# A decode block on one core: the last chunk of the down projection split into three blocks instead of two, with two of the sums made on VectorE

## The chip, the cores and the metric

The kernel runs on one core of a Trainium2 chip. The metric is the time of one execution on the device in microseconds (us); three executions of the kernel before gave 265.24 (the median), 265.24 and 265.53 us.

## What is computed

One decode step of a transformer block for a batch of 8 tokens, all in float32: layernorm, attention over the last 1024 positions of a cached sequence (32 query heads, 4 key/value heads), the output projection, a residual, a second layernorm, a gated GELU layer and a second residual.

```python
B, Sq, D = 8, 1, 1024;  Hq, Hkv, Sk, Dh = 32, 4, 4096, 128;  Df = 3584
W = min(4096, max(256, Sk // 4))                      # 1024
q = (layernorm(x) @ wq) split into 32 heads
p = softmax(q @ k_cache[:, :, Sk - W:].T * Dh ** -0.5);  o = p @ v_cache[:, :, Sk - W:]
h = x + o @ wo
n = layernorm(h)
out = h + (gelu(n @ w_gate) * (n @ w_up)) @ w_down    # w_down: 3584 x 1024
```

## The kernel before

All weights and the cache are read once, in the order of use: query weights, keys, values, output weights, gate and up weights, down weights. Each piece is one DMA on SyncE's queue into a ring in SBUF, and TensorE works on a piece when its semaphore says that it has landed. The order of instructions on each engine is the order in which the program writes them: `run` appends a computation to an engine with the waits that it needs, `move` appends a DMA to a queue (SyncE's unless another is named).

The batch has only 8 rows, so a matmul uses 32 columns of the array. The kernel always keeps four *groups* at work: group r writes PSUM partitions 32r to 32r+31, and matmuls of different groups run side by side.

The down projection (from L410 on) multiplies the activations `at` (28 chunks of 128 of the 3584 inner columns) by the 28 row chunks of `w_down`, each 128 x 1024. The chunks come in loads of 8, 8, 4, 4, 2 and 1 (`PARTS`, `wd0` to `wd5`, L424 to L443); the eight small `w_side` loads carry a part of chunk 19. The last chunk, number 27, comes in blocks of its own (`ENDS`, `we0` and `we1`, L446 to L449). The program writes the loads of the end in the order `wd4`, `wd5`, `we0`, `we1`.

Chunks are taken in pairs at L462: two chunks times two halves of 512 columns give four matmuls of 512 columns, one for each group, all into the bank `ya`. `first = DF // P - TAIL` is 26: pairs go up to chunks 24 and 25. Then VectorE copies `ya` to SBUF (`d1`, L476). What is left is summed in another layout, in which group j holds the output columns 256j to 256j+255. `add` (L481) issues it for two halves of 128 of these columns, the first in bank `acc`, the second in bank `tb`; so it issues eight matmuls of 128 columns. It is called for chunk 26 and then for `d1` with the constant `add2`, which folds the four groups of `ya` into the new layout. Chunk 27 follows at L497, four matmuls for each block. ScalarE copies each half to `o_fin` (L500), and two DMAs store it, `out0` on SyncE's queue (after one more wait for a VectorE memset, L503) and `out1` on ScalarE's.

After that SyncE waits until ScalarE has issued its store, clears the semaphores (L514) and waits for both stores to land (L516).

```python
for q in range(first, last):
    add(lambda j: at[:, q, :], lambda j: rows_of(q)[:, j * QW:(j + 1) * QW], arrived[q], at_ok[1],
        start=(q == first))
add(lambda j: add2[:, j // 2, :], lambda j: d1[:, (j % 2) * QW:(j % 2) * QW + QW], d1_ok)
```

Of the kernel before, what the change touches and what calls it, by code (L numbers as in the profile page):

```python
# [37 lines left out]
class Flow:  # L38
# [42 lines left out]
    def run(self, engine, make, *waits, mark=True):  # L81
        ins = self.start(engine, make, waits)
        if not mark:
            return None
        self.done[engine] += 1
        ins.then_inc(self.own[engine], 1)
        return self.own[engine], self.done[engine]

    def move(self, name, out, src, *waits, engine="sync"):
        s = self.sem(name)  # L90
        self.start(engine, lambda e: e.dma_start(out, src), waits).then_inc(s, 16)  # L91
        return s, 16


def decode_block(nc, x, wq, kt, v, wo, gu, dn, side, ends, outs):
# [9 lines left out]
    run, move = fl.run, fl.move  # L105
# [4 lines left out]
    def sb(name, *shape):  # L110
        return nc.alloc_sbuf_tensor(name, list(shape), F32).ap()
# [15 lines left out]
    def load(src, name, letters, **sizes):  # L127
# [9 lines left out]
    ta, tb, ya = bank("ta", N), bank("tb", N), bank("ya", N)  # L137
    acc = bank("acc", N)
# [12 lines left out]
        out=ident, in_=ident, compare_op=ALU.not_equal, fill=1.0, base=0,  # L151
# [76 lines left out]
    for hf in range(2):  # L228
        w, w_in, wb = wq_t[hf]
        q_ps = (acc, tb)[hf]  # L230
        for c in range(NC):
            for j in range(NQ):
                tok = run("tensor", lambda e, c=c, j=j: e.matmul(  # L233
                    q_ps[32 * j:32 * j + 32, :], xt[c], w[:, c, j * N:(j + 1) * N],
                    start=(c == 0), stop=(c == NC - 1)),
                    w_in, x_ok, mark=(c == NC - 1 and j == NQ - 1))
        free[wb] = tok
        q_sb = sb(f"q{hf}", P, N)
        tok = run("vector", lambda e: e.tensor_scalar(q_sb, q_ps, scale, None, op0=ALU.mult), tok)
        acc_free = tok  # L240
        qt, tok = transposes(ta, q_sb, N // P, tok, ta_free)
# [10 lines left out]
    for hf in range(2):  # L252
        s_ps = big[hf]
        k_t, k_in, wb = load(kt[hf], f"kt{hf}", "s b k", s=2, b=B)
        for b in range(HB):
            for k0 in range(0, W, N):
                for r in range(NQ):
                    s, half = divmod(r, 2)
                    c0 = 32 * b + 160 * half
                    end = b == HB - 1 and k0 + N == W and r == NQ - 1  # L260
                    tok = run("tensor", lambda e: e.matmul(  # L261
                        s_ps[32 * r:32 * r + 32, k0:k0 + N], qz[hf][:, s, c0:c0 + 32],
                        k_t[:, s, half * HB + b, k0:k0 + N],
                        start=(b == 0), stop=(b == HB - 1)), k_in, q_ok[hf], mark=end)
# [31 lines left out]
    for hf in range(2):  # L296
        p_sb, p_ok, share, sh_ok = ps[hf]
        pt = sb(f"pt{hf}", P, KC, P)
        p0, tok0 = transposes(ta, p_sb[:, 0:W // 2], KC // 2, p_ok, ta_free)
# [17 lines left out]
        for b in range(1, HB):  # L317
            tok = run("vector", lambda e: e.scalar_tensor_tensor(
                o_sb, o3[:, b], share[:, b:b + 1], o_sb, op0=ALU.mult, op1=ALU.add), tok)
# [8 lines left out]
    for hf in range(2):  # L328
# [3 lines left out]
        w, w_in, wb = load(wo[hf], f"wo{hf}", "h n", h=2 * REP)  # L332
# [25 lines left out]
    at = sb("at", P, DF // P, 32)  # L358
# [49 lines left out]


    last = DF // P - 1  # L410
    first = DF // P - TAIL
    ring = space.rearrange("p (q n) -> p q n", n=D)
    SLOTS = 2 * BUF // D
    base = place // D
# [4 lines left out]
    def rows_of(q):  # L419
        return ring[:, slot(q)]  # L420
# [22 lines left out]
        q0 += n  # L443
    blocks = []
    c0 = 0
    for i, (n, src) in enumerate(zip(ENDS, ends)):  # L446
        t = rows_of(last)[:, NQ * c0:NQ * (c0 + n)]
        blocks.append((c0, n, t, move(f"we{i}", t, src)))
        c0 += n  # L449


# [2 lines left out]
            ya[32 * ch:32 * ch + 32, :], spread.rearrange("p r b -> p (r b)"),  # L454
            h_sb[:, ch * N:(ch + 1) * N], start=True, stop=False), h_ok, consts, ya_free, mark=False)
    opened = {0, 1}
    for q in range(0, first, 2):
        for i in range(NQ):
            e2, ch = divmod(i, 2)
            r = ch if q in SLOW else i  # L460
            n = N - SIDE_COLS if (q + e2, ch) == (SIDE, 1) else N
            tok = run("tensor", lambda e: e.matmul(  # L462
                ya[32 * r:32 * r + 32, 0:n], at[:, q + e2, :],
                rows_of(q + e2)[:, ch * N:ch * N + n],
                start=(r not in opened), stop=(q == first - 2)),
                arrived[q + e2], at_ok[(q + e2) * P >= SETS[0] * N],
                mark=(q == first - 2 and i == NQ - 1))
# [8 lines left out]
    d1_ok = run("vector", lambda e: e.tensor_copy(d1, ya), tok)  # L476

    cut = ENDS[0]
    halves = [(acc[:, 0:cut], 0, cut), (tb[:, 0:QW - cut], cut, QW)]

    def add(lhs, rhs, *waits, start=False):  # L481

        for d_ps, a, b in halves:
            for j in range(NQ):
                run("tensor", lambda e: e.matmul(  # L485
                    d_ps[32 * j:32 * j + 32, :], lhs(j), rhs(j)[:, a:b], start=start, stop=False),
                    *waits, mark=False)

    for q in range(first, last):
        add(lambda j: at[:, q, :], lambda j: rows_of(q)[:, j * QW:(j + 1) * QW], arrived[q], at_ok[1],  # L490
            start=(q == first))
    add(lambda j: add2[:, j // 2, :], lambda j: d1[:, (j % 2) * QW:(j % 2) * QW + QW], d1_ok)
    o_fin = sb("o_fin", P, QW)
    done = []
    for (c0, n, t, here), (d_ps, a, b) in zip(blocks, halves):
        for j in range(NQ):
            tok = run("tensor", lambda e: e.matmul(  # L497
                d_ps[32 * j:32 * j + 32, :], at[:, last, :], t[:, j * n:(j + 1) * n],
                start=False, stop=True), here, mark=(j == NQ - 1))
        done.append(run("scalar", lambda e: e.copy(o_fin[:, a:b], d_ps), tok))  # L500
# [102 lines left out]
```

## Time and profile before

| | |
|---|---|
| time, median of three executions | 265.24 us (265.24 to 265.53) |
| span of the profiled execution, first to last instruction | 263.8 us |
| the profiled execution's own time | not given apart from its span; 265.24 is 1.44 us above the span |
| TensorE's matmuls busy | 137.9 us, 52% of the span |
| VectorE, ScalarE, GpSimd busy | 23.3, 10.9 and 5.5 us |
| mean granted TensorE clock | 0.819 of full speed, 1.00 in the last 8 us |
| read from and written to HBM | 111.18 and 0.13 MB, 422 GB/s over the span |

In the rows of the trace, PE is a matmul on TensorE and PEld the loading of its weights; a float32 matmul shows as two passes, so four matmuls are "x8". DVE is VectorE and ACT ScalarE. SPq and ACTq are DMA issues on the queues of SyncE and ScalarE, and their duration is that of the issue, not of the transfer. An entry "<-" after an idle time names what ended it. Tile names stand without their numbers: `d` is `d1`, `w` the ring, `out` the output in HBM.

### The profile page before, as it was taken

How to read it: one execution, taken by the hardware profiler on the slowest of the kernel's cores; microseconds unless marked ns; L12 is line 12 of the kernel's file. 1: busy time of each engine (PE TensorE's matmuls, PEld its weight loads, DVE VectorE, ACT ScalarE, POOL GpSimd, SP SyncE). 2: the span in 40 equal slices, each digit the busy share in tenths (PEclk: the TensorE clock that was granted, in tenths of full speed). 3: DMA queues.
4: the chain of work that ended last, by engine and by line, in shares of the span. 5: the costliest groups of instructions: out<-in, count | busy, mean ns of one | idle time of the engine just before them, and what ended most of it. 6: DMA issues, size and time to landing. Idle time of an engine off the chain costs nothing.

```text
span 263.8 us, 2071 instructions
## 1 busy us (share of the span) xinstructions
PE 137.9 (52%) x958; PEld 40.2 (15%) x958; DVE 23.3 (9%) x55; ACT 10.9 (4%) x17; POOL 5.5 (2%) x15
## 2 busy tenths in 40 slices
PE   0015806804905906806707707718509676589875
PEld 0011201201201301301202202112102111123122
DVE  0320100100010020200200100160000200010001
ACT  1110000000010020110000000020000000000000
POOL 8000000000000000000000000000000000000000
PEclk9999975985985895975975956986965979599999
DMA  8998998999799989999998999999899989999995
GB/s 318 482 437 358 477 477 378 420 467 477 328 467 477 420 388 457 470 388 437 447 477 348 460 457 437 398 437 477 360 422 455 477 365 465 412 422 452 390 415 203
DMA packets 3256, 111.44 MB, mean 422 GB/s; under 512 B 392, under 2 KB 648, under 8 KB 1072
## 3 DMA queue, kind: packets, MB, share of 16 engines
q1 hardware_dynamic: 3088, 111.22, 98.0%
q8 instruction: 7, 0.11, 0.2%
q10 hardware_dynamic: 160, 0.10, 0.1%
q14 instruction: 1, 0.01, 0.0%
HBM read 111.18 MB, written 0.13 MB: 422 GB/s over the span
## 4 chain that ended last, share of the span: by engine, by line
DMA 78%; PE 20%; SPq 0%; issue 0%; ACT 0%
DMA w<-gu 20%; DMA w<-wq 16%; DMA w<-kt 12%; DMA w<-wo 11%; DMA w<-v 11%; DMA w<-dn 9%; PE big L376 6%; PE big L261 4%; PE tb L233 4%; PE tb L308 3%; PE ya L336 3%; SPq L91 0%; PE acc L485 0%; ACT o_fin L500 0%; PE tb L485 0%
## 5 line engine op out<-in xcount | busy, mean ns | idle before, releaser
L376 PE MATMUL big<-w,ln_t 128*32 128x512 f32 x224 | 36.1, 730 | 21.6 <-DMA w<-gu 21.6
L261 PE MATMUL big<-w,qz 128*32 128x512 f32 x128 | 18.8, 753 | 20.2 <-DMA w<-kt 20.2
L336 PE MATMUL ya<-w,ot 128*32 128x512 f32 x128 | 18.1, 729 | 19.6 <-DMA w<-wo 19.6
L462 PE MATMUL ya<-w,at 128*32 128x512 f32 (+1 forms) x104 | 16.4, 590 | 3.6 <-DMA w<-dn 3.6
L376 PEld LDWEIGHTS big<-w,ln_t 128*32 128x32 f32 x224 | 9.0, 130 | 47.3 <-issue 25.8
L308 PE MATMUL tb<-w,pt 128*32 128x512 f32 x64 | 9.1, 732 | 9.8 <-DMA w<-v 9.8
L233 PE MATMUL tb<-w,ln_t 128*32 128x512 f32 x64 | 9.2, 743 | 9.2 <-DMA w<-wq 9.2
L308 PE MATMUL acc<-w,pt 128*32 128x512 f32 x64 | 8.5, 694 | 8.6 <-DMA w<-v 8.6
L233 PE MATMUL acc<-w,ln_t 128*32 128x512 f32 x64 | 8.6, 699 | 7.5 <-DMA w<-wq 7.5
L188 PE MATMUL ta<-ident,ln_xn 64*128 64x64 f32 x16 | 2.1, 304 | 19.3 <-DVE ln_xn L214 19.3
L261 PEld LDWEIGHTS big<-w,qz 128*32 128x32 f32 x128 | 4.8, 135 | 33.6 <-issue 23.4
L336 PEld LDWEIGHTS ya<-w,ot 128*32 128x32 f32 x128 | 5.0, 132 | 31.2 <-issue 31.2
L462 PEld LDWEIGHTS ya<-w,at 128*32 128x32 f32 x104 | 4.2, 109 | 15.4 <-issue 10.3
L389 DVE TENSOR_TENSOR hm<-ge,big 128x512 f32<-128x512 f32 (+1 forms) x2 | 1.4, 686 | 56.7 <-PE big L376 56.7
L270 DVE TENSOR_REDUCE nmax<-big 128x1 f32<-128x1024 f32 x2 | 2.5, 1225 | 35.7 <-PE big L261 35.7
L272 ACT ACTIVATE p<-big,nmax 128x1024 f32<-128x1024 f32 x2 | 2.2, 1114 | 78.1 <-DVE nmax L270 78.1
L308 PEld LDWEIGHTS tb<-w,pt 128*32 128x32 f32 x64 | 2.5, 131 | 15.7 <-issue 15.7
L188 PEld LDWEIGHTS ta<-ident,ln_xn 64*128 64x128 f32 x16 | 1.7, 200 | 20.1 <-DVE ln_xn L214 20.1
L233 PEld LDWEIGHTS tb<-w,ln_t 128*32 128x32 f32 x64 | 2.3, 134 | 15.5 <-DMA w<-wq 9.4
L308 PEld LDWEIGHTS acc<-w,pt 128*32 128x32 f32 x64 | 2.4, 126 | 14.1 <-issue 14.1
L233 PEld LDWEIGHTS acc<-w,ln_t 128*32 128x32 f32 x64 | 2.4, 126 | 13.0 <-issue 13.0
L205 ACT ACTIVATE ln_sd<-ln_ve 64x1 f32<-64x1 f32 x2 | 0.4, 203 | 69.3 <-DVE ln_ve L204 69.3
(81 smaller groups left out, 53.3 us busy)
## 6 DMA issues: line engine op xcount, KB each, us to landing
w<-gu SPq DMA_DIRECT2D x2, 6144.0 KB, 23.7
w<-dn SPq DMA_DIRECT2D x2, 4096.0 KB, 27.1
w<-dn SPq DMA_DIRECT2D x1, 2048.0 KB, 20.0
w<-dn SPq DMA_DIRECT2D x1, 1888.0 KB, 24.1
w<-dn SPq DMA_DIRECT2D x1, 1024.0 KB, 22.1
w<-dn SPq DMA_DIRECT2D x1, 512.0 KB, 22.9
w<-ends SPq DMA_DIRECT2D x2, 256.0 KB, 23.1
w_side<-side SPq DMA_DIRECT2D x8, 20.0 KB
```

The lines of the kernel that those rows point to most:

```text
L188: tok = run("tensor", lambda e, i=i: e.transpose(t[:, i, :], src[:, i * P:(i + 1) * P], ident[:rows, :rows]), id_ok, ready, clear, mark=(i ...
L205: tok = run("scalar", lambda e: e.activation(sd, ve, AF.Sqrt), tok)
L233: tok = run("tensor", lambda e, c=c, j=j: e.matmul(q_ps[32 * j:32 * j + 32, :], xt[c], w[:, c, j * N:(j + 1) * N], start=(c == 0), stop=(c ...
L261: tok = run("tensor", lambda e: e.matmul(s_ps[32 * r:32 * r + 32, k0:k0 + N], qz[hf][:, s, c0:c0 + 32], k_t[:, s, half * HB + b, k0:k0 + N ...
L270: tok = run("vector", lambda e: e.tensor_reduce(out=nmax, in_=s_ps, axis=AX.X, op=ALU.max, negate=True), tok)
L272: p_ok = run("scalar", lambda e: e.activation(p_sb, s_ps, AF.Exp, bias=nmax, accum_out=tot), tok)
L308: tok = run("tensor", lambda e: e.matmul(o3[32 * r:32 * r + 32], pt[:, c, 32 * r:32 * r + 32], v_t[:, s, c, half * HB:(half + 1) * HB, :], ...
L336: tok = run("tensor", lambda e: e.matmul(ya[32 * r:32 * r + 32, :], ot[:, 2 * hf * REP + h + e2].rearrange("p r b -> p (r b)"), w[:, h + e ...
L376: tok = run("tensor", lambda e: e.matmul(pair[32 * j:32 * j + 32, s, :], ht[c], w[:, c, j * N:(j + 1) * N], start=(c == 0), stop=(c == NC ...
L389: tok = run("vector", lambda e: e.tensor_mul(hm[:rows], ge[:rows], pair[:rows, 1, :]), tok, g_ok)
L462: tok = run("tensor", lambda e: e.matmul(ya[32 * r:32 * r + 32, 0:n], at[:, q + e2, :], rows_of(q + e2)[:, ch * N:ch * N + n], start=(r no ...
```

## The change

The pairs end with chunk 23 (`FOLD` is 24), and VectorE's copy of `ya` to `d1` comes at that point. Chunks 24 and 25, then `d1` through `add2`, then chunk 26 are summed in the second layout. There, groups 0 to 2 now take their 256 columns in one matmul each into `acc`; group 3 takes its first 128 columns into `acc` and its other 128 into `tb`. One `add` is thus five matmuls instead of eight.

Chunk 27 comes in three blocks: 128 columns of all four groups, the other 128 columns of groups 0 to 2, and the other 128 columns of group 3. Their loads carry 512, 384 and 128 float32 per partition (256, 192 and 64 KB). The first two blocks are multiplied into banks of their own, `ta` and `ya`. ScalarE copies the finished sum in `acc` to SBUF (`most`, in two copies), and VectorE adds `most` and the block's product into `o_fin`. The third block adds to `tb` on TensorE as before, and ScalarE copies that one quarter, 32 partitions of 128. There are three stores: 64 KB and 48 KB on SyncE's queue, 16 KB on ScalarE's. Three memsets of one element on VectorE wait for chunk 26; the one memset on which the first store waited is gone. The host packs `ends` and unpacks `out` to match.

```diff
-ENDS = (128, 128)
-TAIL = 2
+CUT = QW // 2
+ENDS = ((range(0, 4), 0, CUT), (range(0, 3), CUT, QW), (range(3, 4), CUT, QW))
+FOLD = 24
...
-    for i, (n, src) in enumerate(zip(ENDS, ends)):
-        t = rows_of(last)[:, NQ * c0:NQ * (c0 + n)]
-        blocks.append((c0, n, t, move(f"we{i}", t, src)))
+    for i, ((js, a, b), src) in enumerate(zip(ENDS, ends)):
+        n = len(js) * (b - a)
+        t = rows_of(last)[:, c0:c0 + n]
+        blocks.append((t.rearrange("p (j n) -> p j n", n=b - a), move(f"we{i}", t, src)))
         c0 += n
...
-    for q in range(0, first, 2):
+    for q in range(0, FOLD, 2):
...
-    cut = ENDS[0]
-    halves = [(acc[:, 0:cut], 0, cut), (tb[:, 0:QW - cut], cut, QW)]
-
-    def add(lhs, rhs, *waits, start=False):
-
-        for d_ps, a, b in halves:
-            for j in range(NQ):
-                run("tensor", lambda e: e.matmul(
-                    d_ps[32 * j:32 * j + 32, :], lhs(j), rhs(j)[:, a:b], start=start, stop=False),
-                    *waits, mark=False)
-
-    for q in range(first, last):
-        add(lambda j: at[:, q, :], lambda j: rows_of(q)[:, j * QW:(j + 1) * QW], arrived[q], at_ok[1],
-            start=(q == first))
+    def add(lhs, rhs, *waits, start=False, stop=False):
+        for j in range(NQ):
+            w = QW if j < NQ - 1 else CUT
+            tok = run("tensor", lambda e: e.matmul(
+                acc[32 * j:32 * j + 32, 0:w], lhs(j), rhs(j)[:, 0:w], start=start, stop=stop),
+                *waits, mark=(stop and j == NQ - 1))
+        run("tensor", lambda e: e.matmul(
+            tb[96:128, 0:CUT], lhs(NQ - 1), rhs(NQ - 1)[:, CUT:QW], start=start, stop=False),
+            mark=False)
+        return tok
+
+    def row(q, **kw):
+        return add(lambda j: at[:, q, :], lambda j: rows_of(q)[:, j * QW:(j + 1) * QW],
+                   arrived[q], at_ok[1], **kw)
+
+    row(FOLD, start=True)
+    row(FOLD + 1)
     add(lambda j: add2[:, j // 2, :], lambda j: d1[:, (j % 2) * QW:(j % 2) * QW + QW], d1_ok)
+    most_in = row(last - 1, stop=True)
+    assert FOLD + 3 == last
+
+    mark = sb("mark", 1, 3)
+    for i in range(3):
+        run("vector", lambda e: e.memset(mark[:, i:i + 1], 0.0), arrived[last - 1])
+    most = sb("most", P, QW)
+    most_ok = [
+        run("scalar", lambda e: e.copy(most[:, 0:CUT], acc[:, 0:CUT]), most_in),
+        run("scalar", lambda e: e.copy(most[0:96, CUT:QW], acc[0:96, CUT:QW]), most_in)]
+
     o_fin = sb("o_fin", P, QW)
     done = []
-    for (c0, n, t, here), (d_ps, a, b) in zip(blocks, halves):
-        for j in range(NQ):
+    for i, ((js, a, b), (t, here), d_ps) in enumerate(zip(ENDS, blocks, (ta, ya, tb))):
+        k = len(js) * 32
+        direct = i == len(ENDS) - 1
+        for j in js:
             tok = run("tensor", lambda e: e.matmul(
-                d_ps[32 * j:32 * j + 32, :], at[:, last, :], t[:, j * n:(j + 1) * n],
-                start=False, stop=True), here, mark=(j == NQ - 1))
-        done.append(run("scalar", lambda e: e.copy(o_fin[:, a:b], d_ps), tok))
-
-    mark = sb("mark", 1, 1)
-    over = run("vector", lambda e: e.memset(mark, 0.0), blocks[0][3])
-    sent = [move("out0", outs[0], o_fin[:, 0:cut], done[0], over),
-            move("out1", outs[1], o_fin[:, cut:QW], done[1], engine="scalar")]
+                d_ps[32 * j:32 * j + 32, 0:CUT], at[:, last, :], t[:, j - js[0], :],
+                start=not direct, stop=True), here, side_ok, d1_ok, mark=(j == js[-1]))
+        p0 = 32 * js[0]
+        if direct:
+            done.append(run("scalar", lambda e: e.copy(o_fin[p0:p0 + k, a:b], d_ps[p0:p0 + k, 0:CUT]), tok))
+        else:
+            done.append(run("vector", lambda e: e.tensor_add(
+                o_fin[0:k, a:b], most[0:k, a:b], d_ps[0:k, 0:CUT]), most_ok[i], tok))
+
+    sent = []
+    for i, (js, a, b) in enumerate(ENDS):
+        p0, k = 32 * js[0], 32 * len(js)
+        sent.append(move(f"out{i}", outs[i], o_fin[p0:p0 + k, a:b], done[i],
+                         engine="scalar" if i == len(ENDS) - 1 else "sync"))
```

More of the change, by code (lines that the diff above doesn't have):

```diff
@@ L410, in decode_block @@
     last = DF // P - 1
-    first = DF // P - TAIL
     ring = space.rearrange("p (q n) -> p q n", n=D)
@@ L464, in decode_block @@
                 rows_of(q + e2)[:, ch * N:ch * N + n],
-                start=(r not in opened), stop=(q == first - 2)),
+                start=(r not in opened), stop=(q == FOLD - 2)),
                 arrived[q + e2], at_ok[(q + e2) * P >= SETS[0] * N],
-                mark=(q == first - 2 and i == NQ - 1))
+                mark=(q == FOLD - 2 and i == NQ - 1))
             opened.add(r)
@@ L557 @@
     side = side.transpose(0, 2, 1, 3, 4).reshape(8, 4, len(SIDE_ROWS), SIDE_COLS)
-    cuts = [sum(ENDS[:i]) for i in range(len(ENDS) + 1)]
     by_group = rows[-1].reshape(P, NQ, QW)
-    ends = np.concatenate([by_group[:, :, a:b].reshape(-1) for a, b in zip(cuts, cuts[1:])])
+    ends = [by_group[:, js[0]:js[-1] + 1, a:b].reshape(P, -1) for js, a, b in ENDS]
+    sizes = [e.shape[1] for e in ends]
+    ends = np.concatenate([e.reshape(-1) for e in ends])
     arrays = {
@@ L572 @@
     out = nc.dram_tensor("out", (P * QW,), F32, kind="ExternalOutput").ap()
-    cut = P * ENDS[0]
-    outs = [o.rearrange("(p n) -> p n", p=P) for o in (out[0:cut], out[cut:P * QW])]
-    aps["ends"] = [
-        aps["ends"][P * NQ * a:P * NQ * b].rearrange("(p n) -> p n", p=P)
-        for a, b in zip(cuts, cuts[1:])
-    ]
+    outs, f0 = [], 0
+    for js, a, b in ENDS:
+        n = 32 * len(js) * (b - a)
+        outs.append(out[f0:f0 + n].rearrange("(p n) -> p n", n=b - a))
+        f0 += n
+    flat, f0 = aps["ends"], 0
+    aps["ends"] = []
+    for n in sizes:
+        aps["ends"].append(flat[f0:f0 + P * n].rearrange("(p n) -> p n", p=P))
+        f0 += P * n
     flat, f0 = aps["dn"], 0
@@ L598 @@
     flat = r.results[0]["out"].reshape(-1)
-    got = np.concatenate(
-        [flat[:cut].reshape(P, -1), flat[cut:].reshape(P, -1)], axis=1
-    ).reshape(NQ, CP, B, QW)[:, 0]
-    return own(got.transpose(1, 0, 2)).reshape(B, 1, D)
+    got = np.empty((NQ, CP, B, QW), np.float32)
+    f0 = 0
+    for js, a, b in ENDS:
+        n = 32 * len(js) * (b - a)
+        got[js[0]:js[-1] + 1, :, :, a:b] = flat[f0:f0 + n].reshape(len(js), CP, B, b - a)
+        f0 += n
+    return own(got[:, 0].transpose(1, 0, 2)).reshape(B, 1, D)
```

## The prediction, made before the changed kernel ran

> **What bounds the kernel now.** I read the chain of waits of the page first. Nearly all of the span is a load or the matmuls that eat it:
>
> ```profile
> span 263.8 us, 2071 instructions
> ...
> DMA 78%; PE 20%; SPq 0%; issue 0%; ACT 0%
> ```
>
> The change leaves the stream of loads alone up to the last 512 KB, so only the end can move. The time, 265.24 us, is 1.44 us above the span; the page gives no time of the profiled execution itself, so I work with the span and take that 1.44 as fixed. Next the timeline from 256 us on (start, duration, engine and line), from which these rows come:
>
> ```profile
> 237.57 0.91 SPq L91 DMA_DIRECT2D w<-ends  x2
> ...
> 256.31 1.92 PE L462 MATMUL ya<-w,at 128*32 128x512 f32 x16 [0.86 <-DMA w<-dn]
> 256.77 0.13 PEld L462 LDWEIGHTS ya<-w,at 128*32 128x32 f32 x4 [0.30 <-issue]
> 257.20 0.13 PEld L462 LDWEIGHTS ya<-w,at 128*32 128x32 f32 x4 [0.30 <-issue]
> ...
> 258.79 1.06 PE L462 MATMUL ya<-w,at 128*32 128x512 f32 x8 [0.55 <-DMA w<-dn]
> 259.92 0.69 DVE L476 COPY d<-ya 128x512 f32<-128x512 f32 x1 [21.50 <-PE ya L462]
> ...
> 260.06 0.43 PE L485 MATMUL acc<-w,at 128*32 128x128 f32 x8 [0.20 <-DMA w<-dn]
> 260.19 0.24 PEld L485 LDWEIGHTS tb<-w,at 128*32 128x32 f32 x8
> 260.30 0.40 PE L485 MATMUL tb<-w,at 128*32 128x128 f32 x8
> 260.67 0.16 PEld L485 LDWEIGHTS acc<-d,add 128*32 128x32 f32 x8 [0.23 <-DVE d L476]
> ...
> 260.91 0.40 PE L485 MATMUL tb<-d,add 128*32 128x128 f32 x8
> 261.02 0.24 PEld L497 LDWEIGHTS acc<-w,at 128*32 128x32 f32 x8
> 261.13 0.40 PE L497 MATMUL acc<-w,at 128*32 128x128 f32 x8
> 261.30 0.18 PEld L497 LDWEIGHTS tb<-w,at 128*32 128x32 f32 x8
> 261.35 0.40 PE L497 MATMUL tb<-w,at 128*32 128x128 f32 x8
> 261.60 0.27 ACT L500 COPY o_fin<-acc 128x128 f32<-128x128 f32 x1 [22.88 <-PE acc L497]
> 261.82 0.27 ACT L500 COPY o_fin<-tb 128x128 f32<-128x128 f32 x1
> 261.95 0.35 SPq L91 DMA_DIRECT2D out<-o_fin  x1
> 262.11 0.35 ACTq L91 DMA_DIRECT2D out<-o_fin  x1
> ```
>
> From 260.06 on TensorE has one gap: it waits for VectorE's `d1` until 260.67. Without it and with the `d1` step out of the way, TensorE would be done far sooner. But the weights of each block of eight passes are loaded 0.11 us ahead of its matmuls (260.19 for 260.30, 261.02 for 261.13), except those of the very last, 261.30 for 261.35. They came late because the last load had just landed, which the view of the DMA issues confirms (KB each, median us from issue to landing):
>
> ```profile
> w<-dn SPq DMA_DIRECT2D x1, 512.0 KB, 22.9
> w<-ends SPq DMA_DIRECT2D x2, 256.0 KB, 23.1
> ...
> out<-o_fin SPq DMA_DIRECT2D x1, 64.0 KB, 1.6
> out<-o_fin ACTq DMA_DIRECT2D x1, 64.0 KB, 1.6
> ```
>
> The `ends` are issued at 237.57 and, as each issue takes 0.43, at 238.05: they land at about 260.65 and 261.2. I take 260.64 and 261.26, the latter 0.04 ahead of 261.30. So there are two bounds at the end, TensorE's chain and the last load, and they meet within 0.1 us. Removing TensorE's chain alone buys almost nothing; the end is then last load, matmul, copy, store.
>
> **Part by part.** *The loads.* The windows show when the traffic stops (after the engines: clock, mean busy share of the DMA engines, GB/s), and the DMA view of two short windows gives the price of a packet:
>
> ```profile
> 260.40:260.60 0.20, 0.20 (x12) 0.03 (x4) 0.20 (x1) 0.00 (x0) 0.00 (x0) 1.00 0.66 255
> 260.60:260.80 0.20, 0.20 (x8) 0.13 (x8) 0.07 (x2) 0.00 (x0) 0.00 (x0) 1.00 0.28 102
> 260.80:261.00 0.20, 0.20 (x12) 0.20 (x12) 0.00 (x0) 0.00 (x0) 0.00 (x0) 1.00 0.01 0
> ...
> DMA packets 58, 0.11 MB, mean 271 GB/s; under 512 B 5, under 2 KB 5, under 8 KB 58
> q1 hardware_dynamic: 58, 0.11, 70.3%
> ...
> DMA packets 288, 0.13 MB, mean 164 GB/s; under 512 B 32, under 2 KB 288, under 8 KB 288
> q10 hardware_dynamic: 144, 0.07, 27.3%
> ```
>
> The first pair is 260.1 to 260.5, while the blocks of chunk 27 load (2 KB per partition): 53 packets of 2 KB take 70.3% of 16 engines times 0.4 us, 84 ns each. The second is 262.7 to 263.5, the stores (512 B per partition): ScalarE's 128 packets of 512 B, with 16 small ones, take 27.3% of 16 times 0.8 us, 27 ns each. A line through both puts 1.5 KB at 65 ns. A load of 128 partitions gives each of the 16 engines 8 packets. Bytes and order stay, only the second block is cut: 8 x 65 + 8 x 27 = 0.74 instead of 8 x 84 = 0.67 us, so 0.07 later at the end. The second block lands 0.52 after the first, at about 261.15, the third at 261.33. No load of 512-B packets is in the trace. The bounds are 0 (equal bytes) and, were a small load packet as dear as a 2-KB one, 8 x 84 = 0.67 more. I take 0.07, by the store's row, which has the very size. The added issue on SyncE's queue costs 0.43 at 238.5, hidden by 22 us of queued loads.
>
> *`d1`.* Chunks 20 to 23 are done at 256.31 + 1.92 = 258.23; VectorE's copy then runs from about 258.3 to 259.0, while TensorE waits for chunks 24 and 25 (258.79). It is needed after them, at 259.7: hidden with 0.7 to spare; a slower copy would cost only what goes beyond that.
>
> *TensorE.* A 512-column pass holds its group for 0.43 us (256.77, 257.20), so one of 256 holds it 0.21, one of 128 0.11 (the step from 260.19 to 260.30). An `add` is then 2 x 0.21 on groups 0 to 2 and 4 x 0.11 on group 3: 0.43 to 0.44, beside each other, against 0.48 before (from 260.06 to the end of its issue at 260.54). From 258.82: chunk 24 to 259.25, chunk 25 to 259.69, `d1` to 260.12, chunk 26, landed at 260.01, to 260.56. The first end block (260.64) finds TensorE free, and its matmuls run 260.68 to 261.08; the second's 261.19 to 261.59. The third has its weights at 261.37 and two passes on one group from 261.42: 0.11 + 0.27 = 0.38, done at 261.80. That is 0.05 after the old 261.75.
>
> *ScalarE.* `most` can be copied when chunk 26 is through, 260.35 + 0.38 = 260.73: copies of 0.27, 0.22 apart, 260.80 to 261.07 and 261.02 to 261.29. The quarter's copy waits 0.07 for the matmul, as at 261.82, and runs 261.87 to 262.14 (columns set the duration, I assume; 32 partitions instead of 128). Issue at 262.16 against 262.11.
>
> *VectorE.* No add of this shape is in the trace; the nearest rows by form:
>
> ```profile
> L318 DVE SCALAR_TENSOR_TENSOR o<-acc,share,o 128x128 f32<-128x128 f32 x3 | 1.1, 351 | 0.1
> ...
> L389 DVE TENSOR_TENSOR hm<-ge,big 96x512 f32<-96x512 f32 x1 | 0.7, 684 | 26.0 <-PE big L376 26.0
> ```
>
> So 0.35, at most 0.68. The three memsets ahead of the adds wait for chunk 26 (260.01) and are long over. The first add waits for TensorE (261.08) and `most` (261.07): 261.15 to 261.50, store at 261.58. The second: 261.66 to 262.01, store at 262.09, SyncE being free since 261.93. Behind these stores only SyncE's final clearing is queued, which waits for ScalarE's issue anyway. At 0.68 the second store is issued at 262.49 and would be the last, 0.3 later.
>
> *The stores.* Before, the last store is issued at 262.11 and lands 1.6 later by the issues' view; I take 1.63, as the span ends at 263.8 with its landing. Both stores run over each other from 262.8 to 263.4:
>
> ```profile
> 262.60:262.80 0.20, 0.00 (x0) 0.00 (x0) 0.00 (x0) 0.00 (x0) 0.00 (x0) 1.00 0.00 0
> 262.80:263.00 0.20, 0.00 (x0) 0.00 (x0) 0.00 (x0) 0.00 (x0) 0.00 (x0) 1.00 0.81 243
> 263.00:263.20 0.20, 0.00 (x0) 0.00 (x0) 0.00 (x0) 0.00 (x0) 0.00 (x0) 1.00 0.94 287
> 263.20:263.40 0.20, 0.00 (x0) 0.00 (x0) 0.00 (x0) 0.00 (x0) 0.00 (x0) 1.00 0.45 126
> ```
>
> 0.85 us pass before the first packet, about 0.35 from the last packet to landing; the packets of 128 KB lie between. Now 64 KB have gone by 262.7, and 48 + 16 KB follow: 6 + 2 packets of 27 ns on each engine instead of 8 + 8. The last store's own wait and packets shrink from 0.43 to about 0.15: issue at 262.16, landing about 1.35 later, at 263.5. Bounds 1.2 (no packets at all) and 1.63.
>
> The sum: +0.05 until the last issue, -0.28 in the store: -0.23 of 263.8, a time of 265.0 us.
>
> On the store a rule weighs against this. The Trainium skill, "DMA: Bandwidth & Descriptors", section "Anatomy of one DMA", puts a DMA at a fixed 2.0 us or so, mostly completion, plus bytes at 436 GB/s, measured on GpSimd's path. By it 48 KB less save 0.11 us, an estimate from that page, and the sum would be -0.06, 265.2. The measured 1.6 us for 64 KB already lies below its fixed part, so I go by the packets; no row shows a 16-KB store.
>
> **Rivals.** *No gain* (265.2 to 265.3): the time from issue to landing is 1.6 whatever the size, as both stores' rows say. Then 262.16 + 1.63 = 263.79, +0.05. Against it stand the 0.55 us of store packets in the windows. The rule above lies between.
>
> *Slower, by small load packets* (265.6 to 265.9): if the third block's 512-B packets cost 84 ns each on the way in, it lands 0.67 instead of 0.07 later; the end is 0.6 above the forecast, 265.6, and with the full store of 1.63 it is 265.9. It turns slower from 27 + 0.23/8 = 56 ns on. For it: no load of that size was seen. Against: the store's 27 ns.
>
> *Slower, by instruction loading* (265.3). The page of the window 261.9 to 262.3 shows one packet of instructions:
>
> ```profile
> q14 instruction: 1, 0.01, 6.8%
> ```
>
> It takes 6.8% of 16 x 0.4, 0.44 us of one engine, after the loads. SyncE now gets a further load and store to issue; if the packet belongs to SyncE, it is fetched sooner, and among the loads it would hold one engine up by 8 KB, some 4 x 84 = 0.34. That is +0.1.
>
> *Faster by far* (264.6): in the timed executions the `ends` land earlier against TensorE's chain than here, so that its whole 0.6 us goes (260.56 instead of 261.13 when chunk 27 may begin) rather than a part. Against: the last block's late weights in the profile.
>
> **How the numbers follow.** The forecast, 264.8 to 265.1, gets 0.48; no gain 0.20; small packets 0.13, half of it beyond +0.53 us; instruction loading 0.07; faster by far 0.12. A measurement of this kernel tells 0.2%, 0.53 us, from no change (its own runs spread by 0.29). Faster by more is the last rival: 0.12. Slower by more: half of the small packets, 0.06, and 0.05 taken from the forecast for two prices together (0.68 adds with the full store). Same: the rest, 0.77. Range 264.6 to 265.7: it takes in the far gain and all but the top of small packets.
>
> **What would show it.** After: `d1`'s copy near 258.3, no TensorE gap before chunk 26; the quarter's weights near 261.37; ScalarE's store near 262.16, landing in 1.35. Wrong if the third block's weights come after 261.6 (packets), if the last store still takes 1.6, or if the second SyncE store lands last.

## The result: slower by 1.04 us, and the profile after

| | before | after |
|---|---|---|
| median (lowest to highest), six runs each on one chip | 265.24 us (265.21 to 265.53) | 266.28 us (265.83 to 266.47) |
| ratio of after to before | | 1.0031, 95% interval 1.002 to 1.0042 |
| profiled execution: time, span | span 263.8 us | 266.45 us, span 265.1 us |

The forecast was 265.0 us in a range of 264.6 to 265.7. The kernel after is slower by more than the 0.2% that a measurement can tell, and its median lies 0.58 us above the range.

The span of the profiled execution has grown by 1.3 us; this execution took 266.45 us, 0.17 above the median. The page of the kernel after, the span and the chain that ended last:

```profile
span 265.1 us, 2080 instructions
...
DMA 78%; PE 20%; SPq 1%; issue 0%; ACT 0%
DMA w<-gu 20%; DMA w<-wq 15%; DMA w<-kt 12%; DMA w<-wo 11%; DMA w<-v 11%; DMA w<-ends 9%; PE big L377 6%; PE ya L337 4%; PE big L262 4%; PE tb L234 3%; PE tb L309 3%; SPq L92 1%; PE ya L518 0%; ACT o_fin L523 0%; PE tb L518 0%
```

The chain is the one that was forecast: the `ends` land, TensorE multiplies the last block, ScalarE copies the quarter, the store ends the span. Only its date is wrong. The timeline of the kernel after, its last stretch (start, duration, engine, line, and what the engine waited for):

```profile
258.29 1.93 PE L463 MATMUL ya<-w,at 128*32 128x512 f32 x16
...
260.07 0.63 PE L485 MATMUL acc<-w,at 128*32 128x256 f32 x8
...
260.28 0.69 DVE L477 COPY d<-ya 128x512 f32<-128x512 f32 x1 [20.41 <-PE ya L463]
...
260.52 0.61 PE L485 MATMUL acc<-w,at 128*32 128x256 f32 x8
...
261.02 0.63 PE L485 MATMUL acc<-d,add 128*32 128x256 f32 x8
...
261.30 0.08 DVE L506 MEMSET mark<- 1x1 f32 x3 [0.33 <-DMA w<-dn]
...
261.48 0.61 PE L485 MATMUL acc<-w,at 128*32 128x256 f32 x8
...
261.91 0.42 PE L518 MATMUL ta<-w,at 128*32 128x128 f32 x8
262.16 0.27 ACT L509 COPY most<-acc 128x128 f32<-128x128 f32 x1 [22.01 <-PE acc L485]
...
262.42 0.15 PEld L518 LDWEIGHTS ya<-w,at 128*32 128x32 f32 x6 [0.36 <-DMA w<-ends]
...
262.53 0.29 DVE L525 TENSOR_TENSOR o_fin<-most,ta 128x128 f32<-128x128 f32 x1 [1.16 <-ACT most L509]
262.60 0.14 PEld L518 LDWEIGHTS tb<-w,at 128*32 128x32 f32 x2
...
262.84 0.82 SPq L92 DMA_DIRECT2D out<-o_fin  x2
...
263.05 0.26 ACT L523 COPY o_fin<-tb 32x128 f32<-32x128 f32 x1 [0.46 <-PE tb L518]
263.33 0.36 ACTq L92 DMA_DIRECT2D out<-o_fin  x1
```

The memsets wait for chunk 26 and run at 261.30: chunk 26 landed at 261.25, where before it landed at 260.01. All loads from `wd2` (chunks 16 to 19) on are late by as much: chunks 16 to 19 landed at 252.61 for 251.36, chunks 20 to 23 at 257.50 for 256.27, chunks 24 and 25 at 260.02 for 258.74, the three end blocks at 261.86, 262.38 and 262.56 for two at 260.63 and 261.26. The windows of the kernel after show how they are late (after the engines: clock, mean busy share of the 16 DMA engines, GB/s):

```profile
260.80:261.20 0.40, 0.40 (x15) 0.26 (x10) 0.17 (x1) 0.00 (x0) 0.00 (x0) 1.00 0.21 65
261.20:261.60 0.40, 0.40 (x14) 0.40 (x10) 0.08 (x3) 0.00 (x0) 0.00 (x0) 1.00 0.07 26
261.60:262.00 0.40, 0.40 (x18) 0.33 (x12) 0.00 (x0) 0.00 (x0) 0.00 (x0) 1.00 0.06 22
```

A share of 0.06 is one engine of sixteen. Before, the share was down to 0.01 by 261.0. After, one engine works on by itself for about another microsecond with all others done. The trace's landings say the same. A load is split into 16 parts, one for each DMA engine, and its semaphore is raised once for each part that has landed. Of the 16 parts of chunk 26, fifteen land by 260.20 and the last at 261.25, where before the last two landed at 260.00 and 260.01; of the second end block fifteen by 261.30 and the last at 262.38. Each load in which this engine has a part waits for it.

The engine falls behind some 20 us earlier. DMA view of the kernel after, 241.4 to 241.9:

```profile
q1 hardware_dynamic: 5, 0.16, 84.4%
q14 instruction: 1, 0.01, 4.1%
```

This is the packet of instructions, 8 KB, that the prediction found at 261.9 to 262.3, behind the loads. It is now at 241.44, in the middle of them. 4.1% of 16 engines times 0.5 us is 0.33 us on one engine.

The kernel before has late parts too, and they show why this one counts. Its seven packets in row q8 (16 KB, 1.02 to 1.11 us each by the trace) are probably TensorE's, which has 1916 of the 2071 instructions. After each of them, from 46.2 to 255.2, one part more of the following loads lands over 1 us behind the first ones, and four more do so from the load of chunks 16 to 19 on, next to the small `w_side` loads: of chunk 26's parts five land by 258.58 and eleven from 259.62 to 260.01. The five have over 1 us to spare. In the kernel after, one part more is late in the load of chunks 8 to 15 (seven for six), the next to land after the packet at 241.44. In the next load it is ten late parts as before, but one of them is 1.07 behind the other nine. So the engine that the packet held up is, by this count, one that falls behind a second time; the trace doesn't name the engine of a part.

Last load and span both end 1.30 us later. Of that, 0.18 is in all engines (chunk 26's fifteen other parts land by 260.20 instead of 260.01). This is no effect of the changed end, as the first load of the kernel has it already (22.91 for 22.73); in the fourteen profiled executions here that load lands between 22.64 and 23.22. Another 1.06 is the one engine (262.38 less the second block's next-to-last part, 261.30, is 1.08; chunk 26 has 1.05), and 0.06 is the split of the last block. The issue of the last store comes 0.77 us after the last landing, 0.85 before, and its landing takes 1.77 instead of about 1.63; these two cancel within 0.1 us.

### The profile page after: what moved, and what is told of

It reads as the page before. It is cut to its first block, busy times and chain, and to the rows that moved or that the text cites. A ratio compares the mean times of both kernels' runs of the same rounds, so it can differ in the third digit from the quotient of the medians.

```text
span 265.1 us, 2080 instructions
## 1 busy us (share of the span) xinstructions
PE 141.5 (53%) x958; PEld 41.7 (16%) x958; DVE 23.9 (9%) x59; ACT 11.1 (4%) x18; POOL 5.5 (2%) x15
## 4 chain that ended last, share of the span: by engine, by line
DMA 78%; PE 20%; SPq 1%; issue 0%; ACT 0%
DMA w<-gu 20%; DMA w<-wq 15%; DMA w<-kt 12%; DMA w<-wo 11%; DMA w<-v 11%; DMA w<-ends 9%; PE big L377 6%; PE ya L337 4%; PE big L262 4%; PE tb L234 3%; PE tb L309 3%; SPq L92 1%; PE ya L518 0%; ACT o_fin L523 0%; PE tb L518 0%
## 5 line engine op out<-in xcount | busy, mean ns | idle before, releaser
L337 PE MATMUL ya<-w,ot 128*32 128x512 f32 x128 | 18.8, 754 | 20.5 <-DMA w<-wo 20.5
L262 PE MATMUL big<-w,qz 128*32 128x512 f32 x128 | 18.2, 734 | 20.7 <-DMA w<-kt 20.7
L309 PE MATMUL acc<-w,pt 128*32 128x512 f32 x64 | 9.7, 777 | 9.4 <-DMA w<-v 9.4
L234 PE MATMUL acc<-w,ln_t 128*32 128x512 f32 x64 | 9.9, 785 | 7.5 <-DMA w<-wq 7.5
```

Of the source, the lines that this page charges most:

```text
L234: tok = run("tensor", lambda e, c=c, j=j: e.matmul(q_ps[32 * j:32 * j + 32, :], xt[c], w[:, c, j * N:(j + 1) * N], start=(c == 0), stop=(c ...
L262: tok = run("tensor", lambda e: e.matmul(s_ps[32 * r:32 * r + 32, k0:k0 + N], qz[hf][:, s, c0:c0 + 32], k_t[:, s, half * HB + b, k0:k0 + N ...
L309: tok = run("tensor", lambda e: e.matmul(o3[32 * r:32 * r + 32], pt[:, c, 32 * r:32 * r + 32], v_t[:, s, c, half * HB:(half + 1) * HB, :], ...
L337: tok = run("tensor", lambda e: e.matmul(ya[32 * r:32 * r + 32, :], ot[:, 2 * hf * REP + h + e2].rearrange("p r b -> p (r b)"), w[:, h + e ...
```

## The experiments

The theory formed from this: a fetch of instructions among the loads holds up one DMA engine, and everything at the end waits for that engine. Open was what moved the fetch: SyncE's longer program (one load and one store more), as the prediction's rival had it; VectorE's longer program (three memsets for one, two adds, two more waits: 68 instructions for 62, waits counted); or the changed end itself. Rivals without a fetch: the third block's small packets, and the order of loads. All runs are of five rounds, ratios are to the kernel before on the same chip (265.22 to 265.29 us). "Packet" is the 8-KB packet of row q14.

### SyncE's program: three runs

`e1_side_on_act` takes one load off SyncE's queue, in the kernel after:

```diff
-                fl.start("sync", lambda e: e.dma_start(w_side[p0:p0 + 13:4], src), [zero[-1]]).then_inc(
-                    side_in, 16)
+                fl.start("scalar" if h == 7 else "sync", lambda e: e.dma_start(
+                    w_side[p0:p0 + 13:4], src), [zero[-1]]).then_inc(side_in, 16)
```

> The changed kernel with one of the eight small w_side loads issued on ScalarE's queue, so that SyncE issues 28 loads ahead of its stores, as in the kernel before, instead of 29. Instruction theory (SyncE's 8-KB packet of instructions, seen at 261.9 before and at 241.4 after, is fetched at its 29th DMA, and among the loads it holds one DMA engine up by about 1.1 us): the packet is back behind the loads, chunk 26 lands at 260.0 to 260.3 instead of 261.25, the time is 265.2 to 265.5. Rival (three loads, small packets, three stores and VectorE's adds cost the time): all these are unchanged, 266.0 to 266.4.

Measured: 266.02 us, ratio 1.0034 (1.0022 to 1.0045); packet at 239.85, chunk 26 at 260.87.

`e3_third_on_act` moves the 64-KB block, in the kernel after, to ScalarE's queue, where it lands 13 us early, at about 249.4:

```diff
-        blocks.append((t.rearrange("p (j n) -> p j n", n=b - a), move(f"we{i}", t, src)))
+        on_act = i == len(ENDS) - 1
+        blocks.append((t.rearrange("p (j n) -> p j n", n=b - a), move(
+            f"we{i}", t, src, clear if on_act else None, engine="scalar" if on_act else "sync")))
```

> The changed kernel with the third end block loaded from ScalarE's queue: 28 loads on SyncE's queue, and the 64 KB no longer come last. Instruction theory: 265.1 to 265.5, chunk 26 at 260.0 to 260.3. Rival that the small packets of the last load cost the time: also back to 265.3. Rival that stores and adds cost it: 266.0 to 266.4.

Measured: 266.28 us, ratio 1.0036 (1.0024 to 1.0049); packet at 242.13, chunk 26 at 260.96.

`e4_two_blocks` is the kernel after with two end blocks as before, two stores, and two VectorE adds (66 VectorE instructions, SyncE as many DMAs as before):

```diff
-ENDS = ((range(0, 4), 0, CUT), (range(0, 3), CUT, QW), (range(3, 4), CUT, QW))
+ENDS = ((range(0, 4), 0, CUT), (range(0, 4), CUT, QW))
...
```

> The changed kernel with two end blocks instead of three (two loads of 256 KB, two stores of 64 KB); pairs still end with chunk 23 and VectorE still adds the first block, the second is summed on TensorE in all four groups. Instruction theory: 28 loads, 265.1 to 265.4. Rival that the earlier copy, the ScalarE copy and VectorE's add cost the time: 265.8 to 266.4.

Measured: 265.99 us, ratio 1.0025 (1.0014 to 1.0036); packet at 241.69, chunk 26 at 261.50.

So neither SyncE's 29th load nor the third block, its small packets or the third store is needed for the delay: without each of them, and in e4 without all, the packet stays among the loads and the kernel slow.

`e2_before_29_loads` was to be the other side, the kernel before with one load more (`we1` in two DMAs of 64 partitions each):

```diff
-        blocks.append((c0, n, t, move(f"we{i}", t, src)))
+        k = i + 1
+        here = [move(f"we{i}_{h}", t[h * P // k:(h + 1) * P // k], src[h * P // k:(h + 1) * P // k])
+                for h in range(k)]
+        blocks.append((c0, n, t, here))
...
```

> The kernel before with its second end block loaded by two DMAs of 64 partitions each: the same bytes, the same 2-KB packets, one more DMA on SyncE's queue (29 loads). Instruction theory: the packet of instructions comes among the loads, the issue of the last load takes several us, the last loads land 0.5 to 1.1 us later, 265.7 to 266.3. Rival: a load more costs nothing when 22 us of loads are queued, 265.2 to 265.4.

Measured: 265.85 us, ratio 1.0024 (1.0014 to 1.0033), with the packet at 263.08, behind the loads. It is slower by another way. The windows of this kernel:

```profile
258.60:259.00 0.40, 0.00 (x0) 0.00 (x0) 0.00 (x0) 0.00 (x0) 0.00 (x0) 1.00 1.07 425
...
259.40:259.80 0.40, 0.40 (x8) 0.00 (x0) 0.00 (x0) 0.00 (x0) 0.00 (x0) 1.00 0.82 163
```

At 259.4 the engines are busy and move 163 GB/s; packets of 4 KB begun from 259.0 on take 178 to 452 ns, where in the kernel before they take 159 at the median and at most 172. These are the packets of chunk 26, and many engines are slow there, not one: its eleven later parts all land late, from 260.55 to 261.17. The edit may also have changed which DMA engine writes which partitions, which no view shows, so the time of this run does not test the number of loads, and its own cause was not settled. (The profiled execution, 266.32, was the second slowest of ten.) The packet's place does test the theory of SyncE's program: with 29 loads on SyncE's queue it stayed behind the loads.

### VectorE's program alone: three runs

`e5_before_4_vector` is the kernel before, with four memsets of one element at the end of VectorE's program (66 instructions). No load, matmul, copy or store is changed, and nothing waits for them:

```diff
+    more = sb("more", 1, 4)
+    for i in range(4):
+        run("vector", lambda e: e.memset(more[:, i:i + 1], 0.0), mark=False)
```

> The kernel before with four more memsets of one element on VectorE after its last instruction, where VectorE has nothing to do and nobody waits for it. VectorE theory (the 8-KB packet of instructions that all slow variants show near 240 us is VectorE's, and its longer program makes it come among the loads): the packet moves from 261.9 to 239 to 242, one DMA engine lands its part of the last loads about 0.7 to 1.1 us late, 265.7 to 266.2. Rival (the packet belongs to another engine, or the work in the tail is what costs): 265.2 to 265.4.

Measured: 266.0 us, ratio 1.003 (1.0019 to 1.0041), as much as the whole change. The trace of this kernel, asked for the added line, gives the four memsets (ns min/median/max, first and last start in us):

```profile
L506 DVE MEMSET more<- x4: 59/59/59, 261.5 to 261.5; 1x1 f32 x4
```

Its DMA view of 242.1 to 242.6 has the packet of instructions among the loads:

```profile
q14 instruction: 1, 0.01, 4.2%
```

And its windows have the one engine of sixteen (share 0.07 and 0.05) that works on alone:

```profile
260.40:260.80 0.40, 0.26 (x4) 0.00 (x0) 0.07 (x1) 0.00 (x0) 0.00 (x0) 1.00 0.52 199
260.80:261.20 0.40, 0.39 (x16) 0.38 (x16) 0.40 (x1) 0.00 (x0) 0.00 (x0) 1.00 0.07 26
261.20:261.60 0.40, 0.38 (x16) 0.13 (x8) 0.31 (x6) 0.00 (x0) 0.00 (x0) 1.00 0.05 20
```

The memsets run at 261.5, within a quarter of a microsecond, on an engine that nobody waits for. The packet comes 20 us earlier than in the kernel before, at 242.17, and chunk 26 lands at 260.77 for 260.01.

The Trainium skill, "Runtime: NRT & Kernel Launch", section "Instruction fetch mechanics", says that each engine's sequencer fetches its next block through a DMA queue of its own while it executes the current one, and that the cost of crossing a block is "mostly hidden". The first half agrees with the packet on a row of its own, fetched 19 us before the added instructions run. The second does not hold here: it is hidden from VectorE, which has no idle time before the memsets, and not from the loads, where it costs this kernel 0.77 us.

`e7_before_4_scalar` adds four copies of one element to ScalarE's program instead, in the kernel before:

```diff
+    more = sb("more", 1, 4)
+    for i in range(4):
+        run("scalar", lambda e: e.copy(more[:, i:i + 1], ident[0:1, i:i + 1]), id_ok, mark=False)
```

> The kernel before with four more one-element copies on ScalarE while it waits for the end. VectorE theory: no change, packet at 261 to 262, 265.2 to 265.4. Rival that the packet is ScalarE's: packet among the loads, 265.7 to 266.2.

Measured: 265.18 us, ratio 0.9999 (0.999 to 1.0008); packet at 261.95, chunk 26 at 260.04, both as before. So the packet moves with VectorE's program, not with a longer program as such.

`e10_before_3_vector` is e5 with three memsets (65 instructions):

```diff
+    more = sb("more", 1, 3)
+    for i in range(3):
+        run("vector", lambda e: e.memset(more[:, i:i + 1], 0.0), mark=False)
```

> The kernel before with three more one-element memsets on VectorE behind its last instruction (65 instead of 62 and of 66). Packet theory with a limit of 65: the packet stays behind the loads, 265.2 to 265.5. Rival that each further VectorE instruction costs a little: about three quarters of what four cost, 265.8.

Measured: 266.12 us, ratio 1.003 (1.0018 to 1.0041); packet at 242.46, chunk 26 at 261.05. Neither expectation held: there is no limit between 65 and 66, and three memsets cost at least as much as four.

### The change with a shorter VectorE program: four runs

`e8_after_no_memsets` is the kernel after without its three memsets (65 instructions):

```diff
-    mark = sb("mark", 1, 3)
-    for i in range(3):
-        run("vector", lambda e: e.memset(mark[:, i:i + 1], 0.0), arrived[last - 1])
```

> The changed kernel without the three memsets (65 VectorE instructions with waits). VectorE theory, if the limit lies between 62 and 65 as it lies between 62 and 66: unchanged, 265.9 to 266.4; if the limit is at 65 or 66: 265.2 to 265.5, with the packet behind the loads. Rival that the memsets matter by themselves: they are 0.06 us each and off the path, no change.

Measured: 265.79 us, ratio 1.0021 (1.0012 to 1.0029), between the two ranges expected. The loads are on time again: chunk 26 at 260.11, the third block at 261.41. Its timeline has ScalarE's store where the prediction put it, at 262.16:

```profile
262.18 0.36 ACTq L92 DMA_DIRECT2D out<-o_fin  x1
```

The packet is at 262.73 now, among the stores instead of the loads. The DMA issues of this kernel (KB each, us from issue to landing):

```profile
out<-o_fin SPq DMA_DIRECT2D x1, 64.0 KB, 2.5
out<-o_fin SPq DMA_DIRECT2D x1, 48.0 KB, 2.4
out<-o_fin ACTq DMA_DIRECT2D x1, 16.0 KB, 2.1
```

Fifteen of the 16 parts of the 16-KB store are in by 263.82, 1.64 after the issue; the sixteenth makes it 2.1. The other two stores wait for one part as well, 0.94 us in the first and 0.85 in the second, and the second, the 48 KB, lands last, at 264.46: 0.64 after 263.82.

`e6_after_62_vector` has 62 VectorE instructions, as the kernel before: without the memsets, with `d1` and two of the copies of `ot` on ScalarE:

```diff
-            done = run("vector", lambda e: e.tensor_copy(
-                ot[:, h0:h0 + REP], src.unsqueeze(2).to_broadcast([P, REP, CP, B])), tok)
+            dst, src = ot[:, h0:h0 + REP], src.unsqueeze(2).to_broadcast([P, REP, CP, B])
+            done = (run("scalar", lambda e: e.copy(dst, src), tok) if hf == 0 else
+                    run("vector", lambda e: e.tensor_copy(dst, src), tok))
...
-    d1_ok = run("vector", lambda e: e.tensor_copy(d1, ya), tok)
+    d1_ok = run("scalar", lambda e: e.copy(d1, ya), tok)
...
```

> The changed kernel with as many VectorE instructions as the kernel before (62 with its waits, instead of 68): the three memsets are left out, d1 and the two ot copies of the first half of the heads are made by ScalarE. Everything else of the change stays: three blocks, three stores, VectorE's two adds. VectorE theory: packet behind the loads, chunk 26 lands at 260.0 to 260.3, 265.2 to 265.5. Rival: 265.9 to 266.4.

Measured: 266.37 us, ratio 1.0038 (1.0024 to 1.0051). The packet left the loads, at 263.67, and hit the last store. The DMA issues of this kernel:

```profile
out<-o_fin ACTq DMA_DIRECT2D x1, 16.0 KB, 2.6
```

Fifteen parts land by 264.08, the sixteenth at 265.02: 0.94 us for one packet. Some 0.3 us are the loads': the third block landed at 261.67, 0.26 later than in e8, with one part 0.26 behind the others and no packet near; this was not followed up. A number of instructions that is harmless in the kernel before is not so here, since the fetch falls on other DMAs.

`e9_after_65_pad` asked whether VectorE's progress sets the date: e8 with `d1` on ScalarE and one long add, 1.21 us, at the end of VectorE's program (65 instructions again):

```diff
-    d1_ok = run("vector", lambda e: e.tensor_copy(d1, ya), tok)
+    d1_ok = run("scalar", lambda e: e.copy(d1, ya), tok)
...
+    pad = sb("pad", P, D)
+    run("vector", lambda e: e.tensor_add(pad, h_sb, h_sb), mark=False)
```

> The changed kernel with 65 VectorE instructions (no memsets, d1 copied by ScalarE) of which the last is an add of 128 x 1024 elements behind the two adds, whose result nobody reads: it keeps VectorE busy for about 1.2 us, so that the 8-KB packet, which comes 0.7 to 1.4 us after VectorE's last instruction, comes behind the packets of the stores, at 264 or later. Packet theory: with the packet neither among the loads nor among the stores, what is left is the change itself; its last store was issued at 262.18 in the variant without memsets and 15 of 16 engines landed it within 1.64 us, so the span ends near 263.9 and the time is 265.2 to 265.5. Rival (three blocks, stores and adds cost something by themselves): 265.7 to 266.2.

Measured: 265.92 us, ratio 1.0025 (1.0016 to 1.0033). The pad ran from 262.12 to 263.33, and the packet came at 262.57, while it ran: a long last instruction doesn't put the fetch off, and this idea missed. The stores took 2.5, 2.3 and 2.1 us, as in e8.

`e11_after_54_vector` is the test that was missing, the change without the q14 packet in the span. Without the memsets, with `d1`, the four copies of `qz` and all four of `ot` on ScalarE, VectorE has 54 instructions:

```diff
-            ta_free = run("vector", lambda e, s=s: e.tensor_copy(
+            ta_free = run("scalar", lambda e, s=s: e.copy(
...
-            done = run("vector", lambda e: e.tensor_copy(
+            done = run("scalar", lambda e: e.copy(
...
-    d1_ok = run("vector", lambda e: e.tensor_copy(d1, ya), tok)
+    d1_ok = run("scalar", lambda e: e.copy(d1, ya), tok)
...
```

> The changed kernel with 54 VectorE instructions: no memsets, and d1, the four qz copies and the four ot copies made by ScalarE, where they hide beside loads. With 62 the 8-KB packet came at 263.67, still among the last packets of the stores, one of which landed at 265.02 instead of 264.08. Packet theory: eight instructions fewer put the packet behind the stores, at 264.2 or later, or it doesn't come at all; all stores land within 1.65 us, the span ends near 263.9, 265.2 to 265.5. Rival (the change costs something of its own): 265.7 to 266.2.

Measured: 265.42 us, ratio 1.0008 (0.9999 to 1.0017). Its DMA queues and issues have the seven packets of row q8 and no row q14 at all, and all stores are short again:

```profile
q8 instruction: 7, 0.11, 0.2%
...
out<-o_fin SPq DMA_DIRECT2D x1, 64.0 KB, 1.5
out<-o_fin SPq DMA_DIRECT2D x1, 48.0 KB, 1.5
out<-o_fin ACTq DMA_DIRECT2D x1, 16.0 KB, 1.6
```

So the change itself costs +0.2 us at the median, with an interval from nothing to 0.45. The spans recorded for each run say where this lies: the median span of the eleven runs is 263.9 us, as that of the kernel before on the same chip, and 1.5 us lie outside it instead of 1.3. Within the span the change neither gains nor loses, to the 0.1 us in which spans are given. Its profiled execution, 265.83 us, was the slowest of its eleven, with all loads some 0.4 us later from the first one on, so its own landings (chunk 26 at 260.55) say little.

`e12_before_56_vector` is the like for the kernel before, four `qz` copies on ScalarE (56 instructions), to see whether a fetch behind the loads costs nothing:

```diff
-            ta_free = run("vector", lambda e, s=s: e.tensor_copy(
+            ta_free = run("scalar", lambda e, s=s: e.copy(
```

> The kernel before with 56 VectorE instructions instead of 62 (the four qz copies made by ScalarE, hidden beside loads). Packet theory: the packet moves from 261.9, between the loads and the stores, to 262.5 to 263.3, among the stores, and holds up one engine's part of them: 265.6 to 266.2, slower although nothing in the tail is changed. If it moves past 263.4, or does not come, 265.1 to 265.4. Rival (fewer VectorE instructions are never worse): 265.1 to 265.3.

Measured: 265.62 us, ratio 1.0015 (1.0006 to 1.0024), with no packet in the span, chunk 26 at 260.10 and both stores in 1.6 us. The median span of its runs is 263.9, as before, so these copies on ScalarE change nothing in the span; the 0.4 us lie outside the span, 1.7 to 1.8 in all eleven runs, where the kernel before has 1.3 to 1.4 on this chip and the kernel after 1.35 (266.45 less 265.1). The time came out as expected and the mechanism didn't, which is luck. That the fetch runs after the span is possible, and no row shows it.

## Why the prediction was wrong, point by point

**The stream of loads: this step failed.** "The change leaves the stream of loads alone up to the last 512 KB" is true of the program and not of the chip: the last loads land 1.24 us late in chunk 26 already. The sum had +0.07 for the loads; they made 1.30. The runs show why: three memsets on VectorE, in the kernel before, give chunk 26 a delay of 1.04 (e10), four give 0.76 (e5), and four copies on ScalarE none (e7). The prediction's sign of being wrong, third-block weights after 261.6, came true (262.60), but not for the reason it names: the packets were as cheap as forecast, and the whole stream was late.

**The rival "instruction loading".** It had the event, a fetch that moves from behind the loads among them and holds up one engine. It had the wrong engine: the packet follows VectorE's program, not SyncE's (e1, e3, e4 with SyncE's 28 loads as before have it among the loads; so have e5 and e10 with SyncE's program as before; e2 with 29 loads has not). And it was mis-sized: 0.34 us held up, of which +0.1 was left, for a measured 0.6 to 1.1 us, depending on the kernel. Its chance, 0.07, came from that size. The row q14 was in the profile before; asking which engine's program the change makes longer would have named VectorE (+6 instructions) beside SyncE.

**The last store, -0.28: wrong, and hidden by the first.** "Landing about 1.35 later" for 16 KB; measured 1.6 in e11, 1.64 in fifteen of e8's sixteen parts, 1.77 in the kernel after, against 1.63 for 64 KB. The packets did shrink, from 0.39 us (262.99 to 263.38) to 0.22 in e11 (263.53 to 263.75), but the landing came 0.49 after the last of them instead of 0.36, and the first packet 0.91 after the issue instead of 0.88. So a quarter of the bytes took the same time, as the rival "no gain" said. The Trainium skill's rule, "DMA: Bandwidth & Descriptors", section "Anatomy of one DMA", measured on GpSimd's path, that a DMA takes about 2.0 us plus its bytes at 436 GB/s, so that a small one is nearly all fixed cost, fits these runs better than the prediction's packets; its 2.0 us is above what HBM stores take here, 1.5 to 1.8. With 1.63 for 1.35 the sum is +0.05, and the change by itself is the no-gain case: e11 has the same span as the kernel before, 263.9.

**The small load packets: right.** The third block lands 0.18 us after the second, as worked out, and 0.52 lie between first and second; the 512-B load packets have a median of 27 ns, the 1536-B ones 65. That rival, which had the only real weight on the slow side, is refuted.

**TensorE, ScalarE, VectorE: right wherever the loads were on time.** An `add` took 0.43 to 0.46 (starts at 258.87, 259.33, 259.76 and 260.19 in e8) for 0.43 to 0.44, and `d1` was copied from 258.39 there, for 258.3; ScalarE issued at 262.18 in e8 for 262.16; VectorE's adds took 0.29 and 0.28 for 0.35. `d1` was not hidden in the kernel after, as its chunks were late too: TensorE's pairs end at 260.22, the copy at 260.97, and its `add` starts at 261.02. This did not set the end, since the second and third blocks' weights are loaded within 0.04 us of their landing (262.42 for 262.38, 262.60 for 262.56).

**"Faster by far": refuted.** No run lies below the kernel before by more than the measurement can tell; e7, the lowest, is the kernel before with four copies, and the lowest single execution of e11 is 265.24.

**The 1.44 us outside the span, taken as fixed:** 1.3 to 1.35 at the median of every kernel whose single spans were recorded, but 1.5 in e11 and 1.7 in e12.

Open are: why one packet that takes 0.33 us by its record makes the loads 0.6 to 1.1 us late; what exactly sets the date of the fetch (62 instructions: late in all four kernels; 65: early in e10, late in e8 and e9; 66 or more: early in all five); and what lies outside the span in e11 and e12. Where the packet is early, it comes 1.6 to 3.5 us after the copy to `at`, the last VectorE instruction before its wait of some 20 us for the end of the loads; where it is late, it comes behind that wait. No version was faster than the kernel before.

## What to carry to other kernels

In this kernel, which keeps the DMA engines full, packets of instructions travel on the same DMA engines as the data (rows q8 and q14): look in the view of DMA queues for the rows of instruction packets, note when each falls, and ask of every edit which engine's program it lengthens, even by instructions of 59 ns on an idle engine. A load ends with its slowest part, so a busy share of 0.06 at the end of a stream, one engine of sixteen, was a lost microsecond for everyone here. And a store of 16 KB took as long as one of 64 KB (1.62 and 1.63 us): splitting the last store off bought no time.

## What the hardware showed that was not expected

- One 8-KB packet of instructions among saturated loads delays its engine's part of all later loads by 0.6 to 1.1 us, though it occupies the engine for about 0.33 us (4.1% of 16 engines times 0.5 us). Among the stores it costs 0.64 (e8, last landing at 264.46 for 263.82) to 0.94 us (e6).
- After each of the seven 16-KB packets of row q8, in the kernel before as well, one more of a load's 16 parts lands over 1 us late. Such a part costs nothing as long as others are as late: eleven are at the end. The 8-KB packet costs time because its part ends up behind these.
- The same 62 VectorE instructions had their packet at 261.91 in the kernel before, harmless, and at 263.67 in e6, where it held up the last store and with it the end.
- A store of 16 KB takes 1.6 to 1.8 us from issue to landing, one of 64 KB 1.5 to 1.6, where no packet of instructions is among them.
- In the kernel with one load split into two of 64 partitions (e2), 4-KB packets of another load took 178 to 452 ns for over a microsecond, for a median of 159 in the kernel before; why is open.
